# A linear-attention and gated-FFN kernel: second x tile loaded ahead of the weights, packs stored a step later by SyncE, one PSUM tile for numerator and denominator, one Q group ahead of the last KV sum

## The chip, the cores and the metric

The kernel runs on one core of one Trainium2 chip. The metric is the device time of one execution in microseconds (us), median of several; lower is better. The time reported for a run is some 1.8 us longer than the span inside its trace; spans and times are not mixed below.

Engines: PE is TensorE (matmul), PEld its weight load, DVE is VectorE, ACT is ScalarE, POOL is GpSimd, SP is SyncE, which here only issues DMAs. PSUM is the memory that PE writes its sums to.

## The reference

```python
x  = A_x                                     # 2048 x 1024, bf16
xn = layernorm(x)
q, k, v = split(xn @ wqkv)                   # 32 heads of 32
pq, pk  = phi(q), phi(k)                     # phi(t) = (t + 1 if t > 0 else exp(t)) + 1e-6
kv, z   = sum_s pk^T v,  sum_s pk            # per head
s   = ((pq @ kv) / (pq @ z + 1e-6)) @ wo     # num / den, then the projection
g   = silu((silu(B_x @ w_gate) * (B_x @ w_up)) @ w_down)   # B_x is xn here
out = x + s * g
```

No softmax: the attention part is two passes of matmuls with a 32x32 matrix per head in between. The feed-forward part (FFN) has width 3584 and takes two thirds of the time.

## The kernel before

The program has four stages, told apart by what PE does:

1. **KV** (0 to 130 us). For each of 16 token tiles of 128: load x, normalise, transpose, project to k and v in four groups of eight 128x512 matmuls (`Bmm`; each group writes one PSUM bank `kv_ps`), evacuate with phi (`Bev`), and add pk^T v into `kvz` (`C`, the KV sum).
2. **Q(0)** (130 to 148 us). Q of the first block of 512 tokens: one group of eight matmuls per 128 columns (`q_ps`), phi on ACT and DVE, result in `pqT`.
3. **num/den** (148 to 250 us). Per block b and token tile t: eight small matmuls give numerator and denominator (`ND(b,t)`), DVE divides (the evacuation), a DMA transposes the result (`oT`), and PE multiplies by `wo` (`S`). Groups of Q(b+1) and S(b-1) stand between the NDs.
4. **FFN** (250 us to the end).

Alongside runs the preparation of the FFN weights. Each step loads a pack, ACT squares and sums it two steps later, and two steps after that PE adds the sums up (`st1`), DVE scales the pack (`st2`) and POOL makes four differences of it (`T`). The pack is then stored to DRAM.

The start, shortened (the special case of `load_x(0)` and the tests of sizes are cut, most comments are added here):

```python
def load_x(i):
    ...
    x_loads[i] = nc.sync.dma_start(out=x_ap(i), in_=x2[i * P:(i + 1) * P, :])

load_x(0)
load_wkv(0, halves=2)            # 1 MB
nx = 1
for c in range(1, NCH):
    load_x(nx); nx += 1          # 256 KB
    load_wkv(c)                  # 1 MB
...
emit_Bmm(0, 0)
emit_TR(1)                       # PE transpose of x tile 1
ln_pre(2, nc.vector)             # statistics of tile 2, all on DVE
emit_Bev(0, 0)
emit_Bmm(0, 1)                   # needs weight chunk 1
emit_N(2)
emit_Bmm(1, 0)                   # needs chunk 0 and x tile 1
```

The num/den group, shortened. In this stage the kernel divides PSUM into eight tiles of one bank each: `psA` owns three of them, `ps2` five:

```python
psA = p12.enter_context(tc.tile_pool(name="psA", bufs=3, space=PSUM, ...))

def emit_ND(b, t):
    for j in range(NJ):                               # 3, 3 and 2 head groups
        if j < NJ - 1: nd_ps = psA.tile([P, GPT, NDW], FP32, ...)
        else:          nd_ps = ps2.tile([P, GPT, NDW], FP32, ...)
        for gi in range(ng):
            nc.tensor.matmul(nd_ps[:, gi, :], lhsT=pqT[:, g, ttok], rhs=KVZ[:, g, :], ...)
        nc.vector.tensor_scalar(out=rden[:, 0:ng, :], in0=nd_ps[:, 0:ng, P:P + HPG], scalar1=EPS, ...)
        nc.vector.reciprocal(out=rden[:, 0:ng, :], in_=rden[:, 0:ng, :])
        nc.vector.tensor_tensor(out=o_sb[...], in0=nd_ps[...], in1=rden[...], op=ALU.mult)

def nd_item(b, t):
    def f():
        emit_ND(b, t)
        emit_OT(b, t)                                 # DMA transpose
        if b > 0 and (b < NB - 1 or t % 2 == 0):
            prep(1)                                   # one preparation step
    return f
```

An ND takes two tiles of `psA`, which has three: one is spare, so the next ND can begin while DVE is still dividing.

## Time and profile before

764.4 us, median of the first four executions (763.6 to 765.3).

| what | value | view |
|---|---|---|
| PE busy | 752.3 of 762.5 us | busy table of the page |
| matmul time without any gap (estimate; the prediction's 738 is too low) | 747 us | columns of all 3731 matmul records, warm-up and transposes included, at 216 ns for 512 |
| PE idle at 8.8 to 10.8 us | 2.02 us | timeline |
| PE idle at 40.2, 129.7, 152.0, 165.2 us | 0.43, 0.42, 0.98, 0.26 us | timeline |
| DMA engines in the first 20 us | 96% busy, 314 GB/s | stretches |
| DVE in 148 to 166 us | 16.3 of 18 us | stretches |

The first line of the page's busy table: engine, busy us, share of the span, instructions.

```profile
PE 752.3 (99%) x3731; PEld 350.5 (46%) x3731; DVE 551.0 (72%) x1075; ACT 346.6 (45%) x476; POOL 287.7 (38%) x413
```

A PE that is 99% busy by this measure need not be 99% efficient. The Trainium skill ("Perfetto Trace Analysis", Identifying the Most-Contended Engine) says that matmul busy time is not a good measure of how close one is to the roofline, because matmuls are pipelined.

The timeline of PE in the first 21 us of before. Columns: start us, length us, engine, line, operation, out<-in, tile, shape, count, and in brackets the idle time ahead and what ended it.

```profile
6.91 1.90 PE L486 MATMUL kv_ps<-wkv_sb,xnT 128*128 128x512 bf16 x8 [0.20 <-DVE xnT L473]
10.82 0.62 PE L470 MATMUL tr_ps<-ident,xn 128*128 128x128 bf16 x8 [2.02 <-DVE xn L443]
11.28 7.07 PE L486 MATMUL kv_ps<-wkv_sb,xnT 128*128 128x512 bf16 x32
18.80 1.89 PE L486 MATMUL kv_ps<-wkv_sb,xnT 128*128 128x512 bf16 x8 [0.45 <-ACT r_t L151]
```

After the first group PE stands for 2 us until the second x tile has come, been normalised and can be transposed.

The stretches view of the first 20 us (us, then busy time and count of PE, PEld, DVE, ACT, POOL; granted clock; DMA share; GB/s):

```profile
0.00:20.00 20.00, 15.85 (x73) 6.82 (x74) 14.36 (x51) 7.23 (x12) 0.80 (x9) 1.00 0.96 314
```

At 96% the DMA engines have hardly any room left in these 20 us.

The chain of waits near 40 us (start, length, what):

```profile
33.24 7.37 DMA xnT<-xn
40.61 0.05 issue
40.66 1.47 PE kv_ps L486 x6
```

The DMA transpose of x tile 4 took 7.4 us and landed when PE was already waiting.

The timeline of PE from 129 to 166 us, the lines of num/den alone:

```profile
130.14 0.39 PE L508 MATMUL kvz<-v_sb,pk_sb 128*128 128x129 bf16 x4 [0.42 <-ACT v_sb L501]
...
147.72 0.63 PE L632 MATMUL nd_ps<-KVZ,pqT 128*128 128x132 bf16 x8
...
151.64 0.34 PE L632 MATMUL nd_ps<-KVZ,pqT 128*128 128x132 bf16 x3
152.96 0.47 PE L632 MATMUL nd_ps<-KVZ,pqT 128*128 128x132 bf16 x5 [0.98 <-DVE o_blk L640]
...
156.72 0.63 PE L632 MATMUL nd_ps<-KVZ,pqT 128*128 128x132 bf16 x8
...
160.64 0.63 PE L632 MATMUL nd_ps<-KVZ,pqT 128*128 128x132 bf16 x8
...
164.56 0.63 PE L632 MATMUL nd_ps<-KVZ,pqT 128*128 128x132 bf16 x8
```

In block 0 the NDs follow each other after 3.92 us (two Q groups between them), except once: the second one starts its first three matmuls in the spare bank and then waits 1 us for DVE. DVE's three kinds of instruction for an ND, from the groups view (count, then busy us, mean ns, idle before):

```profile
L640 DVE TENSOR_TENSOR o_blk<-nd_ps,rden 128x384 bf16<-128x384 f32 (+1 forms) x48 | 24.6, 513 | 1.7
L639 DVE RECIPROCAL rden<-rden 128x12 f32<-128x12 f32 (+1 forms) x48 | 10.5, 220 | 1.7
L637 DVE TENSOR_SCALAR rden<-nd_ps 128x12 f32<-128x12 f32 (+1 forms) x48 | 7.6, 158 | 4.1 <-PE nd_ps L632 4.1
```

That is 42.7 us for 16 NDs, 2.7 us each. A reciprocal of 12 columns took 228 ns and one of 8 columns 203 ns (groups view by form): the time falls much less than the size, so fewer and larger instructions should save DVE time.

### The profile page before, as it was taken

Reading aid. Unit: us, or ns where it says so; the run is one execution under the profiler, and the core shown is the slowest. Engines: PE = TensorE matmul, PEld = TensorE weight load, DVE = VectorE, ACT = ScalarE, POOL = GpSimd, SP = SyncE. Lnnn points to the kernel's source line nnn. Section 1 sums busy time; section 2 is a strip of 40 time slices with the busy share of each in tenths; the row PEclk is TensorE's granted clock in tenths of the full one; section 3 lists DMA queues with packets and bytes.
Section 4 is the critical chain, followed back from the end, with each engine's and each line's share of the span. In section 5 each row is a group of like instructions: output and inputs, shape, how many; then the busy total and the mean of one; then the engine's idle time right before and its main releaser. Section 6 shows DMA issues by size and latency. Waiting matters only on the chain.

```text
span 762.5 us, 10513 instructions
## 1 busy us (share of the span) xinstructions
PE 752.3 (99%) x3731; PEld 350.5 (46%) x3731; DVE 551.0 (72%) x1075; ACT 346.6 (45%) x476; POOL 287.7 (38%) x413
## 2 busy tenths in 40 slices
PE   7999999999999999999999999999999999999997
PEld 3544444444444444444444444444444444444444
DVE  7788567997666588888889885458676767787335
ACT  3545656788854556666447411132323222211022
POOL 0477599959685265868656000110000000200000
PEclk9999999999999999999999999999999999999999
DMA  9946867769799769898887227398655444530824
GB/s 311 355 93 125 221 241 256 253 224 272 214 314 263 256 230 306 299 347 297 306 312 285 88 86 259 114 344 327 236 189 184 166 165 166 174 144 15 273 87 138
DMA packets 105396, 170.29 MB, mean 223 GB/s; under 512 B 34688, under 2 KB 82176, under 8 KB 94720
## 3 DMA queue, kind: packets, MB, share of 16 engines
q1 hardware_dynamic: 94960, 121.00, 50.3%
q0 software_dynamic: 7936, 44.31, 15.0%
q10 hardware_dynamic: 2448, 4.33, 1.6%
q8 instruction: 29, 0.48, 0.2%
q14 instruction: 23, 0.19, 0.1%
HBM read 111.67 MB, written 50.59 MB: 213 GB/s over the span
## 4 chain that ended last, share of the span: by engine, by line
PE 90%; DVE 5%; DMA 2%; POOL 1%; issue 1%; ACT 1%; SPq 0%; ACTq 0%; DVEq 0%
PE zw L725 25%; PE xb L725 13%; PE dzw L910 12%; PE kv_ps L486 11%; PE s_ps L659 7%; PE yb L725 6%; PE dx L910 6%; PE q_ps L170 4%; PE dy L910 3%; DMA xnT<-xn 1%; PE df L910 1%; PE kvz L508 1%; DMA xp<-in_A_x_dram 1%; DVE o_blk L640 1%; PE nd_ps L632 1%
## 5 line engine op out<-in xcount | busy, mean ns | idle before, releaser
L725 PEld LDWEIGHTS <-w_sb 128*128 128x128 f16 (+1 forms) x1568 | 152.2, 98 | 182.8
L486 PE MATMUL kv_ps<-wkv_sb,xnT 128*128 128x512 bf16 x512 | 114.0, 379 | 1.1 <-ACT r_t L151 0.4
L725 PE MATMUL xb<-xnT,w_sb 128*128 128x512 bf16 x448 | 115.0, 379 | 0.0
L725 PE MATMUL zw<-S,w_sb 128*128 128x512 f16 x448 | 105.8, 379 | 0.0
L725 PE MATMUL zw<-xnT,w_sb 128*128 128x512 bf16 x448 | 105.8, 379 | 0.0
L280 POOL TENSOR_TENSOR w_sb<-w_sb 128x512 f16<-128x512 bf16 x42 | 48.9, 1165 | 95.0 <-DVE w_sb L268 36.3
L247 ACT ACTIVATE w_sb<-w_sb 128x2048 bf16<-128x2048 bf16 x42 | 79.9, 1902 | 5.9 <-DMA w_sb<-in_B_w_up_dram 4.2
L910 PE MATMUL dx<-w_sb,hT 128*128 128x512 bf16 x210 | 79.6, 379 | 0.0
L486 PEld LDWEIGHTS <-xnT 128*128 128x128 bf16 x512 | 48.5, 98 | 56.8 <-DMA xnT<-xn 0.9
L910 PEld LDWEIGHTS <-hT 128*128 128x128 bf16 (+1 forms) x462 | 45.2, 98 | 51.7
L910 PE MATMUL dzw<-w_sb,hT 128*128 128x512 f16 x196 | 58.3, 379 | 0.0
L170 PE MATMUL q_ps<-xnT,wq_sb 128*128 128x512 bf16 x256 | 58.2, 379 | 0.0
L659 PE MATMUL s_ps<-wo_sb,oT 128*128 128x512 bf16 x256 | 57.8, 379 | 0.0
L725 PE MATMUL yb<-S,w_sb 128*128 128x512 f16 x224 | 57.4, 378 | 0.0
L753 DVE SCALAR_TENSOR_TENSOR s<-yb,rc_all,s 128x512 f32<-128x512 f32 x42 | 31.4, 749 | 34.8 <-ACT s L752 34.7
L801 ACT ACTIVATE sg<-cg 128x1024 bf16<-128x1024 f32 x28 | 29.6, 1057 | 57.4 <-DVE cg L794 57.4
L794 DVE SCALAR_TENSOR_TENSOR cg<-zw,rc_all,s 128x1024 f32<-128x1024 f32 x28 | 35.9, 1283 | 26.3 <-PE zw L725 14.0
L850 POOL TENSOR_TENSOR hs<-hT 128x512 f16<-128x512 bf16 x2 | 2.5, 1258 | 132.6 <-ACT sg L801 132.6
L281 POOL TENSOR_TENSOR w_sb<-w_sb 128x512 f16<-128x512 bf16 x42 | 50.1, 1193 | 3.3
L283 POOL TENSOR_TENSOR w_sb<-w_sb 128x512 f16<-128x512 bf16 x42 | 50.8, 1210 | 0.0
L282 POOL TENSOR_TENSOR w_sb<-w_sb 128x512 f16<-128x512 bf16 x42 | 49.8, 1185 | 0.0
L884 POOL DMA_DIRECT2D out_dram<-io x16 | 8.7, 542 | 101.9 <-DVE io L883 101.6
(151 smaller groups left out, 1109.5 us busy)
## 6 DMA issues: line engine op xcount, KB each, us to landing
w_sb<-pk_g SPq DMA_DIRECT2D x27, 1024.0 KB, 6.1
pk_g<-w_sb POOLq DMA_DIRECT2D x14, 1024.0 KB, 5.2
pk_u<-w_sb POOLq DMA_DIRECT2D x14, 1024.0 KB, 5.9
w_sb<-wd SPq DMA_DIRECT2D x14, 1024.0 KB, 5.0
w_sb<-pk_u SPq DMA_DIRECT2D x14, 1024.0 KB, 4.9
w_sb<-wd SPq DMA_DIRECT2D x14, 768.0 KB, 4.5
w_sb<-in_B_w_gate_dram SPq DMA_DIRECT2D x14, 512.0 KB, 5.1
w_sb<-in_B_w_down_dram SPq DMA_DIRECT2D x28, 256.0 KB, 3.4
```

The costliest lines, as they stand in the source:

```text
L170: nc.tensor.matmul(q_ps[:], lhsT=wq_sb[:, dc, g * P:(g + 1) * P], rhs=xn_ap(dc, btok), start=(dc == 0), stop=(dc == DC - 1))
L247: nc.scalar.activation(out=junk, in_=raw_view(key, t), func=ACT.Square, accum_out=asum[:])
L280: nc.gpsimd.tensor_tensor(out=T1, in0=b12, in1=b11, op=ALU.subtract)
L281: nc.gpsimd.tensor_tensor(out=T2, in0=b22, in1=T1, op=ALU.subtract)
L282: nc.gpsimd.tensor_tensor(out=T3, in0=b22, in1=b12, op=ALU.subtract)
L283: nc.gpsimd.tensor_tensor(out=T4, in0=b21, in1=T2, op=ALU.subtract)
L486: mm = nc.tensor.matmul(kv_ps[:], lhsT=xn_ap(dc, tok), rhs=wkv_sb[:, dc, c * CW:(c + 1) * CW], start=(dc == 0), stop=(dc == DC - 1))
L659: mm = nc.tensor.matmul(s_ps[:], lhsT=oT[:, c, ttok], rhs=wo_sb[:, c, cc * CW:(cc + 1) * CW], start=(c == 0), stop=(c == G - 1))
L725: mm = nc.tensor.matmul(out, lhsT=lhs(k), rhs=rhs(k), start=(first and k == 0), stop=(k == HK - 1), skip_group_check=True)
L753: nc.vector.scalar_tensor_tensor(out=s2[:], in0=y_[:], scalar=rc, in1=s1[:], op0=ALU.mult, op1=ALU.add)
L794: nc.vector.scalar_tensor_tensor(out=d12, in0=zw[:], scalar=rc, in1=s2[:, None, :].to_broadcast([P, 2, TB]), op0=ALU.mult, op1=ALU.add)
L910: nc.tensor.matmul(out, lhsT=lhs, rhs=rhs, start=first, stop=lastk, skip_group_check=True)
```

## The change

The intent: start the second tile's work before the big weight transfers, keep the transposes clear of the `wo` loads, cover the last KV sum's wait with a Q group, shorten DVE's part of num/den, and take the stores off POOL. The diff, cut to its core:

```diff
-    psA = ... name="psA", bufs=3
+    psA = ... name="psA", bufs=1
+    def psa_tile(name):
+        t = psA.tile([P, NJ, 512], FP32, name=name, tag="A")        # all three banks
+        return t, t[:, :, 0:GPT * NDW].rearrange("p j (g c) -> p j g c", c=NDW)
 ...
+            if i == 1:
+                x_loads[i] = nc.scalar.dma_start(out=x_ap(i), in_=x2[i * P:(i + 1) * P, :])
+                return
 ...
         load_x(0)
+        load_x(1)
         load_wkv(0, halves=2)
 ...                    # tile 1 is normalised and transposed in halves; its first half and
 ...                    # tile 0 change the engine that copies them out; tile 2 goes earlier
-        for wt, wv in ((wq_sb, wqkv_v), (wo_sb, wo_v)):
+        for c in range(NCC): load_qo(wq_sb, wqkv_v, c)
 ...
                         emit_N(k)
+                        if k - NPE < NCC:
+                            load_qo(wo_sb, wo_v, k - NPE)
 ...
-                    prep(11 * (k + 1) // 16 - 11 * k // 16)
+                    prep(13 * (k + 1) // 16 - 13 * k // 16)
 ...
+        emit_Q(0, 0)
         emit_C(NT - 1)
 ...
-        for g in range(G):
+        for g in range(1, G):
             emit_Q(0, g)
-            if g % 3 == 1:
+            if g == 3:
                 prep(1)
 ...
+            for g in range(G):          # all eight matmuls into one tile of three banks
+                nc.tensor.matmul(nd[:, j, gi, :], ...)
+            ...                         # two additions, one reciprocal, three products
 ...
     def prep_step(between=None):
         ...
+        if prep_out:
+            emit_store(*prep_out.popleft(), nc.sync)     # the pack of the step before
         ...
+        if between is not None:
+            between()                                    # ND and its transpose
         if k3 is not None:
             emit_st2(*k3)
-            emit_T(*k3)
+            emit_T(*k3, later=True)
+            prep_out.append(k3)
```

The two halves of `wo` are loaded behind the norms of tiles 4 and 5 (the loads behind x tile 1 at the start keep their order). Two preparation steps move from the Q(0) stage into the KV stage. The big tile takes all three banks of `psA`, so there is no spare. And the sums that `st1` makes land in an unused column of the ND tile.

More of the change, by code (lines that the diff above doesn't have):

```diff
@@ L78 @@
     p12 = ExitStack()
-    psA = p12.enter_context(tc.tile_pool(name="psA", bufs=3, space=PSUM, reuse_waits="tile"))
+    psA = p12.enter_context(tc.tile_pool(name="psA", bufs=1, space=PSUM, reuse_waits="tile"))
     ps1 = ExitStack()
@@ L268, in emit_sc, with emit_T @@
         nc.vector.tensor_scalar(out=w, in0=w, scalar1=cs_all[:, c:c + 1], scalar2=None, op0=ALU.mult)
-    def emit_T(key, t):
+    def emit_T(key, t, later=False):
         if key[1] == "w":
@@ L283, in emit_T, with emit_store @@
         nc.gpsimd.tensor_tensor(out=T4, in0=b21, in1=T2, op=ALU.subtract)
+        if not later:
+            emit_store(key, t, nc.gpsimd)
+    def emit_store(key, t, eng):
         if key[1] == "w":
@@ L287, in emit_T @@
                 wd_drams[k // 2] = [dram.tile([P, 2, n_, CW], BF16, name="wd%d_%d" % (n_, k // 2)) for n_ in (4, 3)]
+            w = t[:].rearrange("p h a b -> p (h a b)").rearrange("p (q n) -> p q n", n=CW)
             da, db = wd_drams[k // 2]
-            nc.gpsimd.dma_start(out=da[:, k % 2], in_=w[:, 3:7])
-            nc.gpsimd.dma_start(out=db[:, k % 2], in_=w[:, 0:3])
+            eng.dma_start(out=da[:, k % 2], in_=w[:, 3:7])
+            eng.dma_start(out=db[:, k % 2], in_=w[:, 0:3])
             return
         pk = dram.tile([P, 2, DC, FW], BF16, name="pk_%s%d" % key[1:])
-        nc.gpsimd.dma_start(out=pk[:], in_=t[:])
+        eng.dma_start(out=pk[:], in_=t[:])
         pk_drams[key[1:]] = pk
@@ L299, with prep_step @@
     prep_st = deque([None] * 4)
+    prep_out = deque()
     stat_ps = [None]
-    def prep_step():
+    def prep_step(between=None):
         key = prep_q.popleft() if prep_q else None
@@ L313, in prep_step @@
             emit_st1(k3[0], stat_ps[0]())
+        if between is not None:
+            between()
+        if k3 is not None:
             emit_st2(*k3)
-            emit_T(*k3)
+            emit_T(*k3, later=True)
+            prep_out.append(k3)
             if k3[0] in gkeys[0:2]:
@@ L324, in prep_flush @@
     def prep_flush():
-        while prep_q or any(x is not None for x in prep_st):
+        while prep_q or prep_out or any(x is not None for x in prep_st):
             prep_step()
@@ L330 @@
                                                   mybir.EngineType.Activation, mybir.EngineType.Pool}))
-    kvz_ps = [psA.tile([P, GPT, NDW], FP32, name=f"kvz{j}", tag="A") for j in range(NJ)]
+    def psa_tile(name):
+        t = psA.tile([P, NJ, 512], FP32, name=name, tag="A")
+        return t, t[:, :, 0:GPT * NDW].rearrange("p j (g c) -> p j g c", c=NDW)
+    kvz_ps = psa_tile("kvz")[1]
     with ExitStack() as p1:
@@ L366 @@
         load_x(0)
+        load_x(1)
         load_wkv(0, halves=2 if DC % 2 == 0 else 1)
-        nx = 1
+        nx = 2
         for c in range(1, NCH):
+            load_wkv(c)
             if nx < NT:
@@ L372, with load_qo @@
                 nx += 1
-            load_wkv(c)
         for i in range(nx, NT):
             load_x(i)
-        for wt, wv in ((wq_sb, wqkv_v), (wo_sb, wo_v)):
-            for c in range(NCC):
-                nc.sync.dma_start(out=wt[:, :, c * CW:(c + 1) * CW], in_=wv[:, :, c * CW:(c + 1) * CW])
+        def load_qo(wt, wv, c):
+            nc.sync.dma_start(out=wt[:, :, c * CW:(c + 1) * CW], in_=wv[:, :, c * CW:(c + 1) * CW])
+        for c in range(NCC):
+            load_qo(wq_sb, wqkv_v, c)
         PRE_AT = {2: (5, 6), 3: (7, 8), 4: (9, 10), 5: (11, 12), 6: (13, 14), 7: (15,)}
@@ L450, in emit_N @@
             xn_tiles[i] = xn
-            if i == 0:
+            if i < 2:
                 for hh in range(2):
@@ L464, in emit_TR @@
             xn = xn_tiles.pop(i)
-            nh = 2 if i == 0 else 1
+            nh = 2 if i < 2 else 1
             dch = DC // nh
@@ L471, in emit_TR @@
                 dst = xn_ap(slice(hh * dch, (hh + 1) * dch), tok)
-                if i < 2:
+                if i == 1 and hh == 0:
                     nc.vector.tensor_copy(out=dst, in_=tr_ps[:])
@@ L507, in emit_C @@
                 j, gi = divmod(g, GPT)
-                nc.tensor.matmul(kvz_ps[j][:, gi, 0:P + 1], lhsT=pk_sb[:, g * P:(g + 1) * P],
+                nc.tensor.matmul(kvz_ps[:, j, gi, 0:P + 1], lhsT=pk_sb[:, g * P:(g + 1) * P],
                                  rhs=v_sb[:, g, 0:P + 1],
@@ L541 @@
         emit_Bmm(0, 2)
+        emit_TR(2)
         emit_Bev(1, 1)
@@ L547 @@
         ln_pre(4)
-        emit_TR(2)
+        emit_Bmm(2, 0)
         emit_Bmm(0, 3)
@@ L555 @@
             for c in range(NCH):
-                emit_Bmm(i, c)
+                if (i, c) != (2, 0):
+                    emit_Bmm(i, c)
                 if c == 0:
@@ L569 @@
                         emit_N(k)
+                        if k - NPE < NCC:
+                            load_qo(wo_sb, wo_v, k - NPE)
                     for k in PRE_AT.get(i, ())[c // 2:c // 2 + 1]:
                         ln_pre(k)
+        ps1.close()
+        ps2 = p12.enter_context(tc.tile_pool(name="ps2", bufs=5, space=PSUM, reuse_waits="tile"))
+        stat_ps[0] = lambda: ps2.tile([P, 1], FP32, name="st_ps2", tag="B2")[:]
+        emit_Q(0, 0)
         emit_C(NT - 1)
@@ L575 @@
             ng = min(GPT, G - g0)
-            nc.vector.tensor_tensor(out=KVZ[:, g0:g0 + ng, 0:P], in0=kvz_ps[j][:, 0:ng, 0:P],
+            nc.vector.tensor_tensor(out=KVZ[:, g0:g0 + ng, 0:P], in0=kvz_ps[:, j, 0:ng, 0:P],
                                     in1=mask[:, None, :].to_broadcast([P, ng, P]), op=ALU.mult)
             nc.vector.tensor_tensor(out=KVZ[:, g0:g0 + ng, P:P + HPG],
-                                    in0=kvz_ps[j][:, 0:ng, P:P + 1].to_broadcast([P, ng, HPG]),
+                                    in0=kvz_ps[:, j, 0:ng, P:P + 1].to_broadcast([P, ng, HPG]),
                                     in1=sel[:, None, :].to_broadcast([P, ng, HPG]), op=ALU.mult)
-        ps1.close()
-        ps2 = p12.enter_context(tc.tile_pool(name="ps2", bufs=5, space=PSUM, reuse_waits="tile"))
-        stat_ps[0] = lambda: ps2.tile([P, 1], FP32, name="st_ps2", tag="B2")[:]
-        for g in range(G):
+        for g in range(1, G):
             emit_Q(0, g)
-            if g % 3 == 1:
+            if g == 3:
                 prep(1)
@@ L615, with emit_ND @@
         s_tiles = {}
-        def emit_ND(b, t):
+        def emit_ND(b, t, nd):
             pqT = pqT_tiles[b]
@@ L622, in emit_ND @@
             o_sb = o_blks[b][:, t, :]
+            for g in range(G):
+                j, gi = divmod(g, GPT)
+                nc.tensor.matmul(nd[:, j, gi, :], lhsT=pqT[:, g, ttok], rhs=KVZ[:, g, :], start=True, stop=True,
+                                 skip_group_check=True)
+            rden = small.tile([P, NJ * GPT, HPG], FP32, name="rden", tag="rden")
+            for j0, j1, ng in ((0, NJ - 1, GPT), (NJ - 1, NJ, G - (NJ - 1) * GPT)):
+                nc.vector.tensor_scalar(
+                    out=rden[:, j0 * GPT:(j1 - 1) * GPT + ng, :].rearrange("p (j g) h -> p j g h", j=j1 - j0),
+                    in0=nd[:, j0:j1, 0:ng, P:P + HPG], scalar1=EPS, scalar2=None, op0=ALU.add)
+            nc.vector.reciprocal(out=rden[:, 0:G, :], in_=rden[:, 0:G, :])
             for j in range(NJ):
@@ L625, in emit_ND @@
                 ng = min(GPT, G - g0)
-                if j < NJ - 1:
-                    nd_ps = psA.tile([P, GPT, NDW], FP32, name="nd_ps", tag="A")
-                else:
-                    nd_ps = ps2.tile([P, GPT, NDW], FP32, name="nd_ps2", tag="B2")
-                for gi in range(ng):
-                    g = g0 + gi
-                    mm = nc.tensor.matmul(nd_ps[:, gi, :], lhsT=pqT[:, g, ttok], rhs=KVZ[:, g, :],
-                                          start=True, stop=True)
-                    if j == 0 and gi == 0 and t == 0:
-                        marks[("ND", b)] = mm
-                rden = small.tile([P, GPT, HPG], FP32, name="rden", tag="rden")
-                nc.vector.tensor_scalar(out=rden[:, 0:ng, :], in0=nd_ps[:, 0:ng, P:P + HPG],
-                                        scalar1=EPS, scalar2=None, op0=ALU.add)
-                nc.vector.reciprocal(out=rden[:, 0:ng, :], in_=rden[:, 0:ng, :])
                 nc.vector.tensor_tensor(
                     out=o_sb[:, g0 * P:(g0 + ng) * P].rearrange("p (g h e) -> p g h e", g=ng, h=HPG),
-                    in0=nd_ps[:, 0:ng, 0:P].rearrange("p g (h e) -> p g h e", h=HPG),
-                    in1=rden[:, 0:ng, :, None].to_broadcast([P, ng, HPG, DH]),
+                    in0=nd[:, j, 0:ng, 0:P].rearrange("p g (h e) -> p g h e", h=HPG),
+                    in1=rden[:, g0:g0 + ng, :, None].to_broadcast([P, ng, HPG, DH]),
                     op=ALU.mult)
@@ L674, in f, with nd_ot @@
             def f():
-                emit_ND(b, t)
-                emit_OT(b, t)
+                raw, nd = psa_tile("nd")
+                def nd_ot():
+                    emit_ND(b, t, nd)
+                    emit_OT(b, t)
                 if b > 0 and (b < NB - 1 or t % 2 == 0):
-                    prep(1)
+                    stat_ps[0] = lambda: raw[:, 0, 511:512]
+                    prep_step(nd_ot)
+                else:
+                    nd_ot()
             return f
@@ L690 @@
         for b in range(NB):
-            stat_ps[0] = lambda: psA.tile([P, 1], FP32, name="st_ps3", tag="A")[:]
             q = [q_item(b + 1, g) for g in range(G)] if b + 1 < NB else []
@@ L704 @@
         emit_Ssum(passes[0])
+        stat_ps[0] = lambda: psa_tile("st_ps3")[0][:, 0, 511:512]
         prep_flush()
```

## The prediction

> **What bounds it now.** TensorE. The page's busy table has PE busy for 752.3 of 762.5 us. Adding every matmul's own time (an estimate: 512 columns start 216 ns apart in the timeline) gives about 738 us. The rest is the first 1.5 us, the last 4, tiny gaps of about 0.25 us per 20 us everywhere, and a few holes that reordering can fill. The PE timeline and waits show these:
> - 8.8 to 10.8 us: 2.0 us, first transpose of x tile 1 waits for DVE xn
> - 18.2: 0.5 us, kv_ps waits for ACT r_t
> - 40.2: 0.4 us (0.6 start to start), kv_ps waits for an xnT DMA transpose that took 7.4 us behind the wo loads
> - 129.5: 0.4 us (0.6), last KV sum waits for v_sb
> - 152: 1.0 us (1.15), nd_ps waits for DVE o_blk; 165: 0.3 us, same cause.
>
> In all about 5.5 us, 0.7%. Nothing touches the last 500 us (FFN), where PE is full. Over 2% (15 us) is practically excluded.
>
> **Step by step.**
> 1. x tile 1 ahead of the weights. Of the 2.0 us hole I expect only 0.3 us. In the first 20 us the DMA engines are 96% busy at 314 GB/s (windows view). The Trainium skill ("Trainium Kernel Development and Optimization", Key Constraints) says queues of different engines share the same 16 DMA engines; that share agrees. The second weight chunk lands at about 11.1 us in the trace and the second kv_ps group starts at 11.28. x0, x1, chunk 0 and chunk 1 are the same bytes in another order, so chunk 1 still lands near 11. The hole moves behind the transpose and its releaser becomes the DMA wkv_sb. Transposing tile 2 earlier fills the 18 us hole, but its group then waits for ACT: net 0.
> 2. wo loaded between later transposes: the 40 us hole goes, -0.6.
> 3. Q(0,0) before the last KV sum: 1.73 us of matmuls cover the v_sb cast, -0.6.
> 4. One PSUM tile for num/den. DVE per token tile drops from 2.7 us to an estimated 2.2, off the critical path. But before had a spare buffer; now the next ND must wait for the whole evacuation. In block 0 ND repeats every 3.92 us, its evacuation starts 2.6 to 2.8 us after it (behind the ACT/DVE phi of the Q group just before), so it ends at 4.85: 1 us late. After such a stall the next is in time, so I expect stalls at every second ND of block 0, about 2 us in sum, against 1.8 us now. In blocks 1 to 3 spacing is 5.67 us, or evacuation starts at 0.4: no stall. Net 0, from -1.5 to +2.
> 5. Fewer preparation steps in Q(0): included in step 4.
> 6. Stores by SyncE: POOL's period of 5.96 us per pack in 128 to 165 becomes about 5.1, not critical. SyncE will block on POOL, delaying loads and oT transposes by about 1 us, with slack.
>
> Sum: -0.3 -0.6 -0.6 +0 = -1.5 us.
>
> **Predicted: 763.0 us, 80% range 760.6 to 765.4.** Faster by over 2%: 0.01; within 2%: 0.98; slower: 0.01.
>
> **Signs.** Right: kv_ps waits for DMA wkv_sb near 9.5 to 11; no PE hole near 40 and 129; PE waits for DVE o_blk about 1 us between 150 and 166; the span from 252 us on unchanged in length.
>
> **What would make it wrong.** Chunk 1 landing earlier (two queues filling the engines sooner), up to 1.5 us; the ND stalls recurring at each tile and in blocks 1 and 2 (+3 us or more); SyncE blocked so long that ACT or PE waits.

## The result, and the profile after

764.1 us, median of four executions (763.9 to 765.6), against 764.4. The ratio is 1.0, 95% interval 0.9983 to 1.0018. A ratio is the mean time of one kernel's fast runs over that of the other's of the same rounds, so it is not quite the ratio of the medians. In a later job with more rounds (e11) the changed kernel came to 0.9985 of before (0.997 to 0.9999).

The expected gain is there for 20 us of the program and then is not. Starts of the same groups on PE in the two traces, us:

| group | before | after | difference | lost or won since the line above |
|---|---|---|---|---|
| KV sum of tile 1 | 27.05 | 26.11 | -0.94 | -0.94 |
| KV sum of tile 4 | 49.76 | 48.21 | -1.55 | -0.61 |
| ND(0,0) | 147.72 | 145.93 | -1.79 | -0.24 |
| ND(1,0) | 164.56 | 164.43 | -0.13 | **+1.66** |
| first FFN group | 250.27 | 249.69 | -0.58 | -0.45 |
| last matmul | 758.31 | 757.79 | -0.52 | +0.06 |

The KV sum of tile 4 in the timelines of PE, before and after (the experiments count from it):

```profile
49.76 0.62 PE L508 MATMUL kvz<-v_sb,pk_sb 128*128 128x129 bf16 x8
48.21 0.62 PE L530 MATMUL kvz<-v_sb,pk_sb 128*128 128x129 bf16 x8
```

Everything up to ND(0,0) gains 1.8 us; four NDs later 1.7 us of it are gone. The lines that answer to those of before. The busy table:

```profile
PE 752.7 (99%) x3731; PEld 350.4 (46%) x3731; DVE 543.6 (71%) x1026; ACT 348.3 (46%) x479; POOL 269.1 (35%) x382
```

DVE lost 7.4 us and POOL 18.6 us of work, and PE gained nothing by it. The first 21 us of PE:

```profile
7.32 1.90 PE L508 MATMUL kv_ps<-wkv_sb,xnT 128*128 128x512 bf16 x8 [0.38 <-ACT xnT L497]
9.05 0.62 PE L492 MATMUL tr_ps<-ident,xn 128*128 128x128 bf16 x8
10.42 7.07 PE L508 MATMUL kv_ps<-wkv_sb,xnT 128*128 128x512 bf16 x32 [0.75 <-DMA wkv_sb<-in_A_wqkv_dram]
...
20.03 5.34 PE L508 MATMUL kv_ps<-wkv_sb,xnT 128*128 128x512 bf16 x24 [0.33 <-ACT r_t L151]
```

The transpose no longer waits, but the next group now waits for weight chunk 1. The trace's landing records show x tile 1 at 5.3 us (before: 8.1) and chunk 1 at 10.38 (before: 11.06). The stretches view:

```profile
0.00:20.00 20.00, 17.08 (x83) 7.64 (x84) 14.38 (x54) 9.99 (x17) 0.81 (x9) 1.00 0.97 318
```

97% and 318 GB/s: the same saturated engines. The Trainium skill ("DMA: Bandwidth & Descriptors", Queues, rings and completion order) says that a DMA engine takes turns between the queues it has work for. That agrees: x tile 1 on ACT's queue and the first half of chunk 0 on SP's were both issued at 1.20 us and landed at 5.32 and 5.87, where in before that half had landed at 4.90. But x tile 1 was also issued 1.0 us earlier than in before (2.21), so no run tells how much of its 2.8 us comes from the other queue and how much from the earlier place.

The stretch from 127 to 165 us on PE, the lines of the last KV sum and num/den:

```profile
129.55 0.62 PE L530 MATMUL kvz<-v_sb,pk_sb 128*128 128x129 bf16 x8
...
145.93 0.57 PE L652 MATMUL nd<-KVZ,pqT 128*128 128x132 bf16 x7
146.94 0.23 PE L652 MATMUL nd<-KVZ,pqT 128*128 128x132 bf16 x1 [0.44 <-DVE pqT L153]
...
151.79 0.64 PE L652 MATMUL nd<-KVZ,pqT 128*128 128x132 bf16 x8 [1.17 <-DVE o_blk L663]
...
155.73 0.63 PE L652 MATMUL nd<-KVZ,pqT 128*128 128x132 bf16 x8
...
160.39 0.64 PE L652 MATMUL nd<-KVZ,pqT 128*128 128x132 bf16 x8 [0.58 <-DVE o_blk L663]
...
164.43 0.63 PE L652 MATMUL nd<-KVZ,pqT 128*128 128x132 bf16 x8
```

The hole of the last KV sum is gone. In its place the second and the fourth ND wait for the evacuation (o_blk) of the one before, 1.17 and 0.58 us, and the first waits 0.44 us for the last `pqT`. DVE's instructions for an ND are fewer:

```profile
L663 DVE TENSOR_TENSOR o_blk<-nd,rden 128x384 bf16<-128x384 f32 (+1 forms) x48 | 21.7, 506 | 0.6
L659 DVE RECIPROCAL rden<-rden 128x32 f32<-128x32 f32 x16 | 5.7, 353 | 0.6
L656 DVE TENSOR_SCALAR rden<-nd 128x24 f32<-128x24 f32 (+1 forms) x32 | 4.0, 166 | 7.9 <-PE nd L652 7.9
```

31.4 us for 16 NDs, 2.0 us each instead of 2.7. But the evacuation of ND(0,0) starts late, 3.78 us after its ND, and ends 5.80 us after it, just when the second ND can start (timeline of DVE):

```profile
149.71 0.25 DVE L656 TENSOR_SCALAR rden<-nd 128x24 f32<-128x24 f32 x2
150.38 1.35 DVE L663 TENSOR_TENSOR o_blk<-nd,rden 128x384 bf16<-128x384 f32 x3
```

And one new wait of ACT between 120 and 135 us, from the waits view (who waited for whom: us, times, longest):

```profile
ACT w_sb L247 <- DMA w_sb<-in_B_w_down_dram: 1.7, 1, 1.7
```

At 130 us ACT stands 1.7 us for the load of a pack. The phi of the Q groups stands behind it in ACT's order, so DVE too stands still (3.4 us, ended at 133.0 by ACT).

### The profile page after: what moved, and what is told of

It reads as the page before. It is cut to its first block, busy times and chain, and to the rows that moved or that the text cites. A ratio compares the mean times of both kernels' runs of the same rounds, so it can differ in the third digit from the quotient of the medians.

```text
span 762.1 us, 10455 instructions
## 1 busy us (share of the span) xinstructions
PE 752.7 (99%) x3731; PEld 350.4 (46%) x3731; DVE 543.6 (71%) x1026; ACT 348.3 (46%) x479; POOL 269.1 (35%) x382
## 4 chain that ended last, share of the span: by engine, by line
PE 94%; DVE 2%; DMA 1%; ACT 1%; issue 1%; SPq 0%; ACTq 0%; DVEq 0%
PE zw L754 25%; PE kv_ps L508 14%; PE xb L754 13%; PE dzw L939 12%; PE s_ps L682 7%; PE yb L754 6%; PE dx L939 6%; PE q_ps L170 4%; PE dy L939 3%; DMA wkv_sb<-in_A_wqkv_dram 1%; PE kvz L530 1%; PE nd L652 1%; PE df L939 1%; DVE pqT L153 1%; DVE q_ps L147 1%
## 5 line engine op out<-in xcount | busy, mean ns | idle before, releaser
L280 POOL TENSOR_TENSOR w_sb<-w_sb 128x512 f16<-128x512 bf16 x42 | 49.2, 1172 | 118.5 <-ACT s_sb L685 31.4
```

The source lines that it names most:

```text
L280: nc.gpsimd.tensor_tensor(out=T1, in0=b12, in1=b11, op=ALU.subtract)
```

## The experiments

The main theory: **the gain is given back in block 0 of num/den, because one PSUM tile has no spare and the next ND must wait for the whole evacuation of the last.** The rival: **it is given back because SyncE, blocked by the stores that wait for POOL, loads a pack late, so that ACT and DVE come late into num/den.** For runs with several rounds, the ratio and its 95% interval are against before in the same job. The jobs are e1 to e4, e5 to e8 and e9 to e12, on three chips, so medians of different jobs are not compared. In several traces a clock dip or a stray hole in the FFN adds to the span; that is said where it matters. The number that tells most is the time from the KV sum of tile 4 to ND(1,0): 114.80 us before, 116.22 after. It repeats well: 116.33 for the changed kernel in e11, and 114.8 in e4, e9 and e10, which keep num/den as before.

### e1: the three tiles of before put back

```diff
-    psA ... bufs=1        (changed kernel)
+    psA ... bufs=3        (emit_ND, nd_item and the kvz tiles as in before)
```

> The changed kernel with the num/den part of before put back (three PSUM tiles of one bank, reciprocal each; the summed K*V in three tiles too), all else as changed. Theory (the gain of about 1.8 us that PE has at the first num/den group, 145.9 against 147.7 us, is given back because one tile has no spare buffer): the PE holes of 1.3 us at 151 and 0.7 us at 159 shrink to under 0.5 us in sum, the first num/den group of block 1 starts near 162.7 instead of 164.4, total about 762.5. Rival (SyncE, blocked by the stores, makes ACT wait 1.7 us for a pack's load at 130 and DVE runs late into the num/den stage): a hole of about 1 us near 151 stays, total about 764.

Measured: median 763.97 us, ratio 0.9985 (0.9968 to 1.0002). From tile 4's sum to ND(1,0) 114.29 us, 1.9 less than the changed kernel. The PE timeline of e1 shows no idle time ahead of the second and fourth ND:

```profile
151.27 0.79 PE L655 MATMUL nd_ps<-KVZ,pqT 128*128 128x132 bf16 x8
...
159.28 0.63 PE L655 MATMUL nd_ps<-KVZ,pqT 128*128 128x132 bf16 x8
...
163.20 0.63 PE L655 MATMUL nd_ps<-KVZ,pqT 128*128 128x132 bf16 x8
```

The theory's holes went with the single tile, with the SyncE stores still in. The total missed its 762.5 by 1.5 us. The profiled execution (764.19 us) shows two reasons for its own time. The start was less lucky (second `kv_ps` group at 11.12 us, not 10.42), and PE waited once at 245 us, in the S groups of the last block:

```profile
PE s_ps L682 <- DMA oT<-o_blk: 1.0, 1, 1.0
```

That last transpose was issued at 236.05 us, behind a 1 MB load. The executions of e1 ran from 762.1 to 764.5, so it may not be in all of them; this stays open.

### e2: stores by POOL again

```diff
-            emit_T(*k3, later=True)
-            prep_out.append(k3)
+            emit_T(*k3)            # POOL stores at once
```

> The changed kernel with the packs stored by POOL at once, as before. Theory (single tile): the wait of ACT for DMA w_sb at 130 goes from 1.7 us to under 0.3, the first num/den group starts up to 0.9 us earlier, but a hole of 0.9 us or more stays at the second and at one later group of block 0; the start of block 1 moves by under 0.5 us, total 763.5 to 764. Rival (SyncE blocked): both holes go, block 1 starts near 162.5, total about 762.

Measured: median 764.73 us, ratio 0.9996 (0.9978 to 1.0015). The two holes are what they were, to a hundredth:

```profile
151.74 0.64 PE L651 MATMUL nd<-KVZ,pqT 128*128 128x132 bf16 x8 [1.17 <-DVE o_blk L662]
...
160.34 0.64 PE L651 MATMUL nd<-KVZ,pqT 128*128 128x132 bf16 x8 [0.58 <-DVE o_blk L662]
```

So the rival falls as the cause of these holes. A small share stays with it: from tile 4's sum to ND(1,0) took 115.71 us, 0.5 less than the changed kernel, because PE's small hole near 137 is gone and ND(0,0) waits 0.45 us (start to start) for `pqT` in place of 0.60. One detail of the theory fell as well: ACT still waited 2.4 us for a pack's load, now from 136.5 to 138.9 us, so SyncE's stores move that wait and are not its only cause. In this run SP waited for the stores to finish before it could reuse their buffers (19.4 us in four waits between 110 and 150; before 18.6). What is left as a suspect is that 13 instead of 11 steps in the KV stage ask for packs faster than they can be supplied, whoever stores them. e7 tests that.

### e3: num/den ahead of the phi of the Q group before it

The evacuation was late because on DVE it stood behind the phi of the Q group that PE had just finished, which first needs three ACT instructions. In block 0 the order of emission can be turned round; PE's order stays:

```diff
             for k, f in enumerate(body):
+                if b == 0 and k in at:
+                    ev = emit_Q(b + 1, k, later=True)   # the matmuls alone
+                    nd_item(b, at.index(k))()
+                    ev()                                # then phi
+                    continue
                 f()
```

> The changed kernel, but in block 0 the num/den group and its evacuation are put ahead of the phi of the Q group that stands just before it on PE, so that the evacuation starts about 1.7 us earlier. Theory: evacuation ends about 3 us after its group began, the next comes after 3.9, so the holes at 151 and 159 (1.3 and 0.7 us) go, block 1 starts near 162.3, total about 762.0. Rival: DVE still late at the first group, hole of over 0.8 us at 151 stays, block 1 starts after 163.5.

Measured: median 762.39 us, ratio 0.9971 (0.9956 to 0.9986). From tile 4's sum to ND(1,0) 114.16 us; the evacuation of the second to fourth ND starts 0.85 to 0.91 us after its ND and ends at 2.9, that of the first starts at 1.85 and ends at 3.88 (in the changed kernel the first ends at 5.80 and the third, which starts at 2.58, at 4.61). The NDs behind the first follow without idle time:

```profile
150.62 0.63 PE L656 MATMUL nd<-KVZ,pqT 128*128 128x132 bf16 x8
...
154.55 0.63 PE L656 MATMUL nd<-KVZ,pqT 128*128 128x132 bf16 x8
...
158.47 0.63 PE L656 MATMUL nd<-KVZ,pqT 128*128 128x132 bf16 x8
...
162.42 0.63 PE L656 MATMUL nd<-KVZ,pqT 128*128 128x132 bf16 x8
```

The evacuation of the second ND on DVE:

```profile
151.53 0.25 DVE L660 TENSOR_SCALAR rden<-nd 128x24 f32<-128x24 f32 x2
152.20 1.35 DVE L667 TENSOR_TENSOR o_blk<-nd,rden 128x384 bf16<-128x384 f32 x3
```

The single tile is kept, its 0.7 us per ND on DVE is kept, and the holes are gone: what was missing was not DVE throughput but the place of the evacuation in DVE's order. The Trainium skill ("Perfetto Trace Analysis", Optimization Strategy) says that the same gap, repeating, can mean that PSUM ran out for the next tile. These runs agree, with a twist: the gap here came at every second ND (1.17, none, 0.58, none), because a group that starts late finds the next evacuation earlier relative to itself (1.25 and 1.84 us after the delayed second and fourth ND, 2.58 after the third).

### e4: the start of the change alone, on before

```diff
+            if i == 1: x_loads[i] = nc.scalar.dma_start(...)
+        load_x(1)                                  # ahead of the weights
         ... and the halves and earlier transposes of the change
```

> Before with the start of the change alone: second x tile on the ACT queue ahead of the weights, its norm and transpose in halves, tile 2 transposed earlier. Theory: a hole of about 0.9 us before the second kv_ps group, released by DMA wkv_sb, in place of 2.0; the kv_ps stage is ahead by 0.9 us at 26 us, and stays so to the end: total about 763.5. The hole of 0.6 us near 39 (xnT transpose behind wo) stays. Rival (nothing of the start is kept): total 764.4, same PE times as before at 126 us.

Measured: median 764.61 us, ratio 0.9999 (0.9982 to 1.0016). In the trace the hole before the second group was 1.4 us, not 0.9, the KV sum of tile 1 came at 26.75 us (0.3 ahead of before) and that of tile 4 at 49.01 (0.75 ahead). ND(1,0) was still 0.75 ahead. In the FFN, PE idled 1.04 us just before 333.9 us and 0.40 us just before 347.5 us, where the profile of before shows no idle time. So the start's gain reaches the num/den stage, but it is small beside what else varies, and the timing could not tell it from nothing.

### e5: the single tile alone, on before

```diff
-    psA ... bufs=3   ->   +    psA ... bufs=1     (emit_ND and nd_item of the change; POOL stores)
```

> Before with the single num/den PSUM tile alone (one tile of three banks, two additions and one reciprocal on DVE instead of three each; the sum column of the packs in the same tile); all else as before. Theory (no spare buffer): in before the first evacuation starts 4.2 us after its group, so with one tile it ends near 6.4 us and the second group starts about 2.5 us late instead of 1.15; one more hole of about 0.7 us two groups on; block 1 starts 1.5 to 2 us later than in before (near 166 instead of 164.6), total 765.5 to 766.5. DVE is busy about 7 us less. Rival (the 0.5 us saved on DVE per group is worth more than the buffer): block 1 starts no later than 164.6, total 764.2 or less.

Measured: median 768.49 us, ratio 1.0043 (1.003 to 1.0056): slower, clear of noise.

```profile
153.51 0.64 PE L632 MATMUL nd<-KVZ,pqT 128*128 128x132 bf16 x8 [2.18 <-DVE o_blk L643]
...
163.79 0.64 PE L632 MATMUL nd<-KVZ,pqT 128*128 128x132 bf16 x8 [0.58 <-DVE o_blk L643]
```

The evacuation of ND(0,0) started 4.2 us late as in before, and the second ND waited 2.2 us for it. DVE's busy time fell by 7.7 us to 543.3, so 7.7 us less of DVE work did not make up for the lost spare. From tile 4's sum to ND(1,0) took 118.53 us, but 1.7 us of that are a dip of the granted clock to 0.83 between 150 and 160 us (15 Q matmuls took 5.30 us in place of 3.62); without it 2.0 us more than before, the 1.5 to 2 that the theory expected. The total was 2 us above the expected range. The profiled execution has another 1.0 us of waiting for an `oT` transpose near 250, as in e1, and three of the five executions ran at a granted clock of 0.997 or less.

### e6: another start, on e3

PE waits for chunk 1 although it could work on x tile 1 with chunk 0. This run turns the two groups round, and takes the statistics of tile 2 from DVE to POOL so that phi is not held up:

```diff
         emit_TR(1)
-        ln_pre(2, nc.vector)
+        ln_pre(2)                  # POOL
         emit_Bev(0, 0)
-        emit_Bmm(0, 1)
-        emit_N(2)
         emit_Bmm(1, 0)
+        emit_Bev(1, 0)
+        emit_Bmm(0, 1)
+        ...                        # N(2) and TR(2) later
```

> The run before with num/den ahead of phi, and at the start the other token tile's group on the same weight chunk put second, ahead of the group that needs weight chunk 1; the statistics of tile 2 finished on POOL instead of DVE, so that phi is not held up; tile 2 transposed later. Theory (chunk 1's landing bounds the start, not x tile 1): the wait for DMA wkv_sb falls from 0.7 us or more to 0, the second kv_ps group starts at 9.9 to 10.0 us, the hole of 0.5 us near 19 goes too, PE is 0.9 us ahead at 25 us (third tile's KV sum near 25.2 instead of 26.1); total about 761.5. Rival (the start is bound by evacuation on ACT and DVE): a wait for ACT r_t of 1 us or more appears before 22 us and the gain at 25 us is under 0.3.

Measured: median 761.94 us, ratio 0.9958 (0.9945 to 0.9972). The wait for the weights is gone:

```profile
9.64 10.53 PE L512 MATMUL kv_ps<-wkv_sb,xnT 128*128 128x512 bf16 x47 [0.27 <-DVE xnT L499]
```

Six groups run through without a hole, and the KV sum of tile 1 (the text above calls it the third tile's) came at 24.98 us, 1.2 before e3's. So the start was bound by chunk 1's landing (10.32 us here, 10.38 in the changed kernel): PE now has other work until it lands. The profiled execution (763.1 us) lost 2.4 us in the FFN near 330; see below.

### e7: one preparation step moved out of the KV stage, on e3

```diff
-                    prep(13 * (k + 1) // 16 - 13 * k // 16)
+                    prep(12 * (k + 1) // 16 - 12 * k // 16)
...
-                if b > 0 and (b < NB - 1 or t % 2 == 0):
+                if (b, t) == (0, 2) or b > 0 and (b < NB - 1 or t % 2 == 0):
```

> The run before with num/den ahead of phi, with one of the 13 preparation steps of the KV stage moved into block 0 of the num/den stage. Theory (13 steps in the KV stage outrun POOL, so that a pack's load comes late and ACT, then DVE, stand still around 130): ACT's waits of 1 to 2 us for w_sb between 120 and 132 fall under 0.5 us in sum, the q_ps hole of 0.74 us at 136.8 goes, block 1 starts near 161.8 instead of 162.4. Total about 761.8. Rival (the moved step makes ACT late in block 0): a hole of over 0.5 us near the third or fourth num/den group, no gain.

Measured: median 761.42 us, ratio 0.9952 (0.9939 to 0.9966). ACT's waits for `w_sb` between 120 and 135 us are gone from the list, the `q_ps` hole near 137 (0.74 us start to start in e3) too, and from tile 4's sum to ND(1,0) took 113.45 us, 0.7 less than e3. ND(0,0) no longer waits for `pqT`; in exchange the small matmul that adds up a pack's sums ahead of ND(1,0) waits 0.20 us:

```profile
145.85 0.63 PE L656 MATMUL nd<-KVZ,pqT 128*128 128x132 bf16 x8
...
161.93 0.16 PE L255 MATMUL nd<-asum,ones 128*128 128x1 bf16 x1 [0.20 <-DVE o_blk L667]
161.95 0.71 PE L656 MATMUL nd<-KVZ,pqT 128*128 128x132 bf16 x8
```

So ACT's stop at 130 came from packing 13 steps into the KV stage. The loads themselves did not come earlier: they land at 125.96 and 130.44 us here and at 125.80 and 130.33 in the changed kernel, where ACT starts on them within 0.2 us; in e7 it starts at 128.76 and 136.21. What was wrong was the time at which ACT asked. By inference (no run moves the step alone in the changed kernel) this cost the changed kernel its two small holes, measured start to start: 0.36 us near 137 and 0.60 us at ND(0,0).

### e8 and e12: the three together

The edits of e3, e6 and e7 in one kernel, run in two jobs.

> Num/den ahead of phi, the other start and the moved preparation step together. Theory: the three add, 762.4 less 0.9 less 0.6, about 760.9 us.

> The combination (num/den ahead of phi, the other start, one preparation step moved) again beside the changed kernel: 0.995 of before and of the changed kernel, 760.5 us; no hole over 0.5 us before 250 us.

Measured: e8 median 760.37 us, ratio 0.9949 (0.9935 to 0.9962); e12 median 760.48 us, ratio 0.9936 (0.9922 to 0.995). This version beats before by 4 to 5 us in both jobs and the changed kernel by 3.6 us (760.48 against 764.11 in the same job). Within the noise the parts add (760.9 was expected): e6's 1.2 us and e7's 0.7 us at 25 and 161 us are both there in the traces (KV sum of tile 1 at 25.05, ND(1,0) at 160.61), though single executions differ by up to 2 us elsewhere.

### e11: the changed kernel again

> The changed kernel again, for more rounds, beside the next run. Both theories: 0.999 to 1.0 of before, 764 us; holes of 1.3 and 0.7 us at the second and fourth num/den group of block 0 again; the wait for DMA wkv_sb near 10 between 0.7 and 1.6 us, as it varied in the other runs.

Measured: median 764.11 us, ratio 0.9985 (0.997 to 0.9999). The holes at the second and fourth ND were 1.33 and 0.74 us again (start to start), ND(1,0) at 164.63 us.

### e9 and e10: the two remaining parts alone, on before (one look each)

```diff
e9:  wo loaded after the norms of tiles 4 and 5
e10: emit_Q(0, 0) ahead of emit_C(NT - 1)
```

> Before with the two halves of wo loaded after the norms of tiles 4 and 5 instead of ahead of them; all else as before. Theory (the DMA transpose of tile 4 stands behind the wo loads on the DMA engines): it lands 3 to 4 us after its issue instead of 7.4, the PE hole of 0.6 us at 40 goes, the KV sum of the fourth tile comes 0.6 us earlier relative to that of the second. Rival (it is late because its norm is late): the hole stays.

> Before with Q(0,0) ahead of the last KV sum alone. Theory: the PE hole of 0.58 us at 129.5 goes, but it is taken back within 25 us: DVE and ACT are behind in the Q stage of before (first evacuation of num/den starts 4.2 us after its group), so block 1 starts at most 0.3 us earlier than in before. Rival: block 1 starts 0.6 us earlier.

Measured, e9: 767.25 us, one execution with a granted clock of 0.91 in its first 20 us, so its time says nothing. Its trace does: the transpose of tile 4 was issued at 34.75 and landed at 37.99, 3.2 us later, and PE had no hole. The landing records of the four kernels with `wo` ahead show what it was bound by. In before, e4, e5 and e10 it was issued at 33.24, 32.94, 32.52 and 34.32 and landed at 40.61, 39.86, 40.15 and 40.46, each time 0.9 us after the second half of `wo` (39.67, 38.94, 39.21, 39.51). In the changed kernel it was issued at 32.30 and landed at 35.51. So the theory holds, but the hole is not a constant: with `wo` still ahead it was 0.9 us (start to start) in e5, where PE came to it 0.7 us earlier than in before, and nothing in e10, where PE came a microsecond later.

Measured, e10: 767.33 us, one execution, with 2.5 us of holes in the FFN. The hole at the last KV sum went (ND(0,0) 97.37 us after tile 4's sum, before 97.96), and at ND(1,0) the distance is 114.80 us, exactly that of before. The 0.6 us were taken back within one block, as expected: PE came sooner to a DVE that was no faster.

### What varied by itself

Seven of the twelve traces (e2, e4, e6, e8, e9, e10, e12) have 0.9 to 2.5 us of holes (start to start) between 328 and 348 us, in the FFN, which the others lack. They occur with and without each part of the change. In e8 the ACT engine waited there for the load of a raw weight:

```profile
ACT w_sb L251 <- DMA w_sb<-in_B_w_up_dram: 7.1, 2, 5.8
```

Why that load is sometimes late was not tried. It is the likely reason why medians of a few executions scatter by 1 to 2 us.

## Why the prediction was right or wrong

The time, 764.1 us, lies in the predicted range (760.6 to 765.4), and nothing moved by 2%. The four signs came true: the wait for `wkv_sb` at 10.42, no hole near 40 and 129, a wait of 1.17 us for o_blk at 151.8, and 508.1 us from the first FFN group to the last matmul against 508.0. The sum of -1.5 us was too hopeful by about 1 us (-0.52 at the last matmul). That it came so near is in part luck: the start gave 0.6 us more than booked, and from tile 4's sum to the FFN the change lost 1.0 us where 0.6 us of gain was booked; and a range of 4.8 us would also have held no change at all. Term by term:

1. **x tile 1 ahead: mechanism right, size short.** The hole moved behind the transpose and its releaser became the weights, as the text said. "Chunk 1 still lands near 11" was off by a little in this trace: it landed at 10.38, and the gain at 26 us was 0.94 us, not 0.3. (It landed at 10.3 to 11.1 in the ten traces with x tile 1 ahead and at 10.4 to 12.5 in the four without.) Over all traces the second group started at 10.42 to 11.12 us with the changed start (seven traces) and at 10.54 to 12.71 with that of before (four), with means of 10.74 and 11.72, so the gain is perhaps 1 us; the ranges overlap, and one of the four had a lowered clock. The claim that the landing bounds the start is shown by e6, where turning two groups round took the wait to nothing. The small ACT wait for tile 2's group came as predicted (0.33 us).
2. **wo later: right.** -0.61 us between the sums of tiles 1 and 4; e9 shows why.
3. **Q(0,0) ahead: the hole went, the gain did not last.** "-0.6" was booked as if it reached the end. e10 shows that alone it is worth 0.59 us at ND(0,0) and nothing at ND(1,0).
4. **One PSUM tile: mechanism right, net wrong.** The prediction named the lost spare, the evacuation end at 4.85 us against 3.92, and stalls at every second ND, "about 2 us in sum". The holes that wait for o_blk are 1.33 and 0.74 us start to start, 2.07 us. What failed is the other side of that sum, "against 1.8 us now. Net 0": steps 3 to 5 together cost 1.66 us between ND(0,0) and ND(1,0) and won 0.24 before it. In before only 1.15 us of waiting lay in that stretch; another 0.4 lay right after ND(1,0), where the change does win 0.45. And ND(0,0) itself took 0.60 us longer, waiting for `pqT`, which I had not counted. e5 shows the tile alone to cost about 2 us of PE time in this stage (clock dip taken off), e1 and e3 show it removed by three tiles or by another order.
5. **"Included in step 4" was wrong by omission.** I counted the steps taken out of Q(0) as relief for DVE and not the two steps added to the KV stage. With them ACT asked for a pack before it had landed and stopped for 1.7 us at 130. e7 shows it: one step moved, 0.7 us won.
6. **SyncE stores: right in what matters.** POOL's period per pack fell from 5.96 to 5.0 us (5.1 predicted), and PE saw nothing of it. The warning that SyncE blocks long enough to stop ACT looked true in the trace, but e2 shows a stop of 2.4 us, some 8 us later, with POOL's stores; what SyncE's stores cost PE before ND(1,0) was at most the 0.5 us by which e2 was better there.

## What to carry to other kernels

When a change takes a buffer away to save instructions, compare the end of the consumer's work, counted from the producer's start, with the producer's period: here 5.8 us (first ND) and 4.6 us (third) against 3.9 decided the case, and the 0.7 us of DVE time saved per group did not. If the consumer is late because it stands behind other work in its engine's order, move it forward before giving it more buffers. A saving ahead of a stage that is bound by another engine is kept only as far as that stage; look for it at the next boundary, not where it was made.

## What the Trainium skill lacked or had wrong

- "DMA: Bandwidth & Descriptors", Issuing engines are not separate DMA queues: it says that several issuing engines save only the time to issue, which is true of bandwidth (314 and 318 GB/s here). It does not say in that place that a small load on another queue can land ahead of larger ones issued at the same time: x tile 1 on ACT's queue landed at 5.3 us, 512 KB of weights issued with it on SP's at 5.9. (Before, on SP's queue and issued 1.0 us later, it landed at 8.1; queue and order were not tried apart.)
- The same page, DMA Transpose (X-bar): the section has constraints and another one of the page a bandwidth, but neither has a time to land behind other traffic. Here a 256 KB transpose landed 3.2 us after its issue (e9, changed kernel) and 6.1 to 7.6 us after it behind two 1 MB loads of the same queue (before, e4, e5, e10).
- "Perfetto Trace Analysis", Optimization Strategy: its consistent bubbles need not repeat at each period. With one PSUM tile the gap came at every second group, 1.17 and 0.58 us.
- No page that I read tells how much the landing of the same load varies from one execution to the next: the wait for the second weight chunk was 0.7 to 1.5 us in seven traces of the same start.
